# Fused attention and mixture of experts: the weight preparation of six experts moves from the attention into the first token pass, whose second layer becomes plain

## The chip, the cores and the metric

The program runs on one core of one Trainium2 chip. The metric is device time in microseconds (us) of the whole program; lower is better. Three runs of the kernel before gave 1906.63, 1915.39 and 1919.79 us (median 1915.39). One further run was executed under the hardware profiler: 1914.67 us, with a span of 1912.9 us from its first to its last instruction.

## The reference

Causal attention with a decaying bias for 4 batches, 8 heads, 576 positions, head size 64; its output, as 2304 tokens of 512 numbers, goes through eight experts, all of which see every token:

```python
scores = scale * q @ k.T                      # (4, 8, 576, 576), causal
attn   = softmax(scores + min(-(cum_i - cum_j), 0))
x      = (attn @ v) laid out as (2304, 512)
P      = exp(x @ w_gate - max)                # (2304, 8)
for _ in range(8):                            # Sinkhorn: rows, then columns
    P /= P.sum(1) + 1e-9;  P /= P.sum(0) + 1e-9;  P *= N / E
for e in range(8):
    h    = max(x @ w1[e], 0)                  # (2304,512) @ (512,1024)
    out += P[:, e:e+1] * (h @ w2[e])          # (2304,1024) @ (1024,512)
```

## The kernel before

**Numbers.** Every factor is kept as a high part (a cast) and a low part (original minus cast), and a product is three matmuls: high by high, high by low, low by high. A "split" is therefore a cast on ACT and a subtraction on POOL or DVE (helper `sub`, L234; additions L237).

**Attention** (L671 to L712) runs over 80 slots (batch, head pair, row tile), software-pipelined. Between the slots, `fill` drips in matmuls of expert 0, computed plainly (`g1_half` L130, first layer; `g2_chunk` L159, second layer), and `prep` drips in jobs.

**The jobs** prepare the first-layer weights of experts 1 to 7. A unit is a quarter of an expert (256 of 1024 hidden columns), so there are 28. For each, `w1_prep` (L239) loads the raw weights, forms four sums `t13`, `t24` (tile `sb`) and splits three raw blocks and four sums into a tile `w7`, which one DMA stores to the DRAM tensor `w1d`. `w7` and the raw tile `sa` have one buffer each.

**Seven products for eight.** Experts 1 to 7 run in three passes of 768 tokens. Both layers multiply 2x2 blocks with seven products in place of eight, as Strassen and Winograd do. The first layer needs the prepared weights and four sums of token blocks S1 to S4, which `x_sums` (L289) makes from the token blocks in DRAM (`xd`) and stores there. `step1` (L851) is one product of a unit: six matmuls of 384 columns, weights loaded from `w1d` five steps ahead (`load_w1`). Its seventh step also forms sums of the hidden activations: four `clip_op` on DVE and four splits (`plain_split`). `step2` (L951) is one product of the second layer for 128 tokens: twelve matmuls of 256 columns; an expert has 21 of them in a pass, and 28 `step1`. The sums of the second-layer weights are made by `w2_prep` (L269) in the first pass and stored to `w2d`; all second-layer operands are split again for each pass (`split_w2` L931).

**What stands between attention and pass 0.** After the slots, the jobs left over and `x_sums` for pass 0 run (L717 to L720); the attention's pools close; SP, the queue that issues nearly all DMAs in order, is given the seven token loads (`load_x`, L985) and five weight loads, and then the loads of the remaining raw weights of expert 0 (`w_load_early`, L620, tile `wraw`, split at L102/L103). Expert 0's last visits 12 to 15 (batch 3) run beside the Sinkhorn steps (L993).

**Order.** The framework schedules instructions with a timeline simulation of its own; program order is a priority. Each engine then executes its list in order, and a wait holds up all behind it.

Of the kernel before, what the change touches and what calls it, by code (L numbers as in the profile page):

```python
# [14 lines left out]
P = 128  # L15
# [19 lines left out]
TP = 384  # L35
# [3 lines left out]
WOPS = ["11", "21", "22", "T1", "T3", "T2", "T4"]  # L39
XRAW = ["11", "12", "21", "22"]  # L40
# [4 lines left out]
def fused_kernel(ctx: ExitStack, tc: tile.TileContext, qT, kT, v, s, w_gate, wu, out):  # L45
# [193 lines left out]
    def w1_prep(pool, u):  # L239
# [4 lines left out]
        t13 = pool.tile([P, 2, 2, P], F32, name="sb", tag="sb", bufs=2)  # L244
        t24 = pool.tile([P, 2, 2, P], F32, name="sb", tag="sb", bufs=2)
# [19 lines left out]
        parts(5, 2, t24)  # L265
        nc.sync.dma_start(out=w1d[u], in_=w7.bitcast(F32))
        yield

    def w2_prep(pool, u):  # L269

        e, n = divmod(u, UPE)
        r = pool.tile([P, 2, DM], F32, name="sa", tag="sa")
        nc.sync.dma_start(out=r.rearrange("p f d -> p (f d)"), in_=wu[u, :, 1024:2048])
        yield
        t13 = pool.tile([P, 2, DH], F32, name="sb", tag="sb", bufs=2)
        t24 = pool.tile([P, 2, DH], F32, name="sb", tag="sb", bufs=2)
        sub(t13, r[:, :, DH:], r[:, 0, :].rearrange("p (j d) -> p j d", d=DH))
        yield
        sub(t24[:, 0], t13[:, 0], r[:, 1, DH:])
        add(t24[:, 1], t24[:, 0], r[:, 1, :DH])  # L280
        for o, t in ((0, t13), (2, t24)):
            nc.sync.dma_start(
                out=w2d[e][o : o + 2, :, n, :].rearrange("t p d -> p t d"), in_=t
            )
        yield

    XS = 192

    def x_sums(pool, p, k, th, eng):  # L289

        ts = slice(th * XS, (th + 1) * XS)
        x = pool.tile([P, 4, 2, XS], F32, name="sa", tag="sa")
# [3 lines left out]
        ta = pool.tile([P, XS], F32, name="sc", tag="sc", bufs=2)  # L296
        tb = pool.tile([P, XS], F32, name="sc", tag="sc", bufs=2)

        def parts(o, src):
            t = pool.tile([P, 2, XS], F32R, name="sb", tag="sb", bufs=2)  # L300
            nc.scalar.copy(t[:, 0], src)
            sub(t[:, 1], src, t[:, 0].bitcast(F32), eng)
            nc.sync.dma_start(out=xd[p, o][:, :, k, ts], in_=t.bitcast(F32))
# [14 lines left out]
        ta = pool.tile([P, XS], F32, name="sc", tag="sc", bufs=2)  # L318
        add(ta, x[:, 1, 0], tb, eng)
        add(ta, ta, x[:, 1, 1], eng)  # L320
        parts("S4", ta)
        yield
# [325 lines left out]
    def fill(ti):  # L648
# [7 lines left out]
    PREP0, PREP1 = 10, NS - 2  # L656
    jobs = chain(
        [w1_prep(stage, u) for u in range(UPE, NU)]
    )
    njobs = 5 * (NU - UPE)  # L660
    done = [0]

    def prep(ti):
        due = njobs * (ti - PREP0 + 1) // (PREP1 - PREP0)
        while done[0] < min(due, njobs):
            next(jobs, None)
            done[0] += 1

    xs0 = chain([x_sums(stage, 0, k, th, nc.vector) for k in range(2) for th in range(2)])
# [47 lines left out]
    for _ in jobs:  # L717
        pass
    for _ in xs0:
        pass  # L720
    actx.close()

    late = ctx.enter_context(tc.tile_pool(name="late", bufs=1, reuse_waits="tile"))
    ps1 = ctx.enter_context(
# [100 lines left out]
    hops = {}
    hp = []
# [3 lines left out]

    def relu_split(n, o, z):
        t = hp[0].tile([P, 2, TP], F32R, name="h", tag="h", bufs=32)
# [18 lines left out]
    def step1(si):  # L851
        load_w1(si + LEAD1)
        n, o = steps1[si]
        w = w1s.pop(si)
        idx, ui = divmod(n, UPE)
        p = items[idx][0]
# [56 lines left out]

    PROD = ["11", "T1", "T2", "21", "T3", "22", "T4"]
    HOF = {"11": "11", "T1": "S1", "T2": "S2", "21": "12", "T3": "S3", "22": "S4", "T4": "22"}
    steps2 = [(idx, o) for idx in range(NI) for o in PROD]
    r2, w2s = {}, {}
# [67 lines left out]
    for o in XOPS:  # L985
        load_x(0, o)
# [92 lines left out]
```

## Time and profile before

| | |
|---|---|
| profiled execution | 1914.67 us, span 1912.9 us |
| busy: PE, DVE, ACT, POOL | 1702.7, 1307.1, 906.1, 1131.2 us |
| stretch 50 to 425 us (attention) | PE 328.28 of 375 us busy, clock 0.93 |
| stretch 452 to 542 us | PE 2.36 of 90 us busy |
| stretch 650 to 1100 us (pass 0) | PE 415.19 of 450 us busy |
| stretch 1100 to 1900 us (passes 1, 2) | PE 794.67 of 800 us busy |

Busy shares are means over stages with different limits, so the table goes by stage. PE is TensorE; the granted clock is a share of 2.4 GHz, averaged over the stretch.

### The profile page before, as it was taken

How to read it: one execution, taken by the hardware profiler on the slowest of the kernel's cores; microseconds unless marked ns; L12 is line 12 of the kernel's file. 1: busy time of each engine (PE TensorE's matmuls, PEld its weight loads, DVE VectorE, ACT ScalarE, POOL GpSimd, SP SyncE). 2: the span in 40 equal slices, each digit the busy share in tenths (PEclk: the TensorE clock that was granted, in tenths of full speed). 3: DMA queues.
4: the chain of work that ended last, by engine and by line, in shares of the span. 5: the costliest groups of instructions: out<-in, count | busy, mean ns of one | idle time of the engine just before them, and what ended most of it. 6: DMA issues, size and time to landing. Idle time of an engine off the chain costs nothing.

```text
span 1912.9 us, 33715 instructions
## 1 busy us (share of the span) xinstructions
PE 1702.7 (89%) x11865; PEld 1623.9 (85%) x11865; DVE 1307.1 (68%) x2424; ACT 906.1 (47%) x1946; POOL 1131.2 (59%) x993
## 2 busy tenths in 40 slices
PE   5799887994068989989889999999999999999998
PEld 4578776884068989989889999999999999999998
DVE  6668556654326857657767787777787677877775
ACT  5777637653124434434444544444444544444442
POOL 4888677666044666668976454445545444545454
PEclk9799997997579999999999999999999999999999
DMA  6888858875678788877768765665668756656552
GB/s 158 249 261 287 263 208 293 268 263 198 208 284 292 230 263 247 254 249 251 252 219 316 252 186 180 184 186 177 188 187 294 253 175 187 186 179 190 179 181 101
DMA packets 232888, 429.35 MB, mean 224 GB/s; under 512 B 21584, under 2 KB 110160, under 8 KB 229104
## 3 DMA queue, kind: packets, MB, share of 16 engines
q1 hardware_dynamic: 232400, 426.60, 69.5%
q8 instruction: 95, 1.56, 0.3%
q10 hardware_dynamic: 320, 0.59, 0.1%
q14 instruction: 73, 0.60, 0.1%
HBM read 327.01 MB, written 94.81 MB: 221 GB/s over the span
## 4 chain that ended last, share of the span: by engine, by line
PE 49%; DMA 16%; DVE 12%; POOL 12%; issue 6%; SPq 2%; ACT 2%; POOLq 0%; DVEq 0%; ACTq 0%
PE c L869 19%; PE zz L963 12%; PE y L963 8%; DVE s L847 3%; POOL w2o L234 3%; DMA rawq<-qT 3%; DMA sa<-wu 3%; DVE h L234 2%; PE g L167 2%; POOL sb L234 2%; DMA w1d<-w 2%; PE g L138 2%; POOL w L234 2%; POOL h L234 2%; DMA sa<-xd 2%
## 5 line engine op out<-in xcount | busy, mean ns | idle before, releaser
L234 POOL TENSOR_TENSOR w2o<-r,w2o 128x512 fp32r<-128x512 f32 x294 | 419.5, 1447 | 416.1 <-ACT w2o L935 416.1
L869 PE MATMUL c<-xS,w1o 128*128 128x384 f32 x2016 | 423.2, 343 | 21.6 <-DVE z L237 10.8
L963 PE MATMUL zz<-w2o,h 128*128 128x256 f32 x3024 | 424.9, 283 | 9.8 <-POOL w2o L234 6.3
L963 PEld LDWEIGHTS zz<-w2o,h 128*128 128x128 f32 x3024 | 406.6, 189 | 12.4 <-POOL w2o L234 7.8
L869 PEld LDWEIGHTS c<-xS,w1o 128*128 128x128 f32 x2016 | 344.8, 191 | 29.2 <-DVE z L237 14.2
L963 PE MATMUL y<-w2o,h 128*128 128x256 f32 x2268 | 313.8, 284 | 14.6 <-POOL w2o L234 6.8
L963 PEld LDWEIGHTS y<-w2o,h 128*128 128x128 f32 x2268 | 297.8, 189 | 22.8 <-DVE a L978 10.1
L869 PE MATMUL c<-x,w1o 128*128 128x384 f32 x1512 | 306.1, 337 | 4.0 <-ACT c L900 2.7
L833 ACT ACTIVATE h<-z 128x384 fp32r<-128x384 f32 x252 | 131.0, 525 | 296.4 <-DVE z L237 292.1
L869 PEld LDWEIGHTS c<-x,w1o 128*128 128x128 f32 x1512 | 256.5, 188 | 5.4 <-ACT c L900 3.5
L234 POOL TENSOR_TENSOR h<-s,h 128x384 fp32r<-128x384 f32 x168 | 203.3, 1217 | 70.5 <-ACT h L842 69.6
L842 ACT CAST h<-s 128x384 fp32r<-128x384 f32 x336 | 168.0, 513 | 124.7 <-DVE s L847 123.1
L834 DVE SCALAR_TENSOR_TENSOR h<-z,h 128x384 fp32r<-128x384 f32 x252 | 184.4, 740 | 57.9 <-ACT h L833 55.6
L847 DVE SCALAR_TENSOR_TENSOR s<-z,c 128x384 f32<-128x384 f32 x168 | 150.5, 896 | 87.7 <-ACT c L900 87.7
L935 ACT CAST w2o<-r 128x1024 fp32r<-128x1024 f32 x147 | 153.7, 1046 | 86.6 <-PE y L963 56.6
L234 DVE TENSOR_TENSOR h<-s,h 128x384 fp32r<-128x384 f32 x168 | 177.1, 1070 | 3.7 <-ACT h L842 3.1
L978 DVE SCALAR_TENSOR_TENSOR a<-zz,prob,a 128x256 f32<-128x256 f32 x252 | 119.9, 477 | 86.0 <-PE zz L963 85.2
L978 DVE SCALAR_TENSOR_TENSOR a<-y,prob,a 128x256 f32<-128x256 f32 x252 | 113.2, 477 | 85.2 <-PE y L963 84.9
L847 DVE SCALAR_TENSOR_TENSOR s<-z,s 128x384 f32<-128x384 f32 x168 | 165.0, 982 | 2.4
L234 POOL TENSOR_TENSOR sb<-sa 128x512 f32<-128x512 f32 x56 | 74.7, 1334 | 148.0 <-DMA sa<-wu 142.7
L237 DVE TENSOR_TENSOR z<-c,t 128x384 f32<-128x384 f32 x252 | 136.6, 548 | 32.4 <-PE c L869 28.8
L505 ACT ACTIVATE T<-T,mn 128x128 f32<-128x128 f32 (+2 forms) x144 | 83.6, 581 | 50.0 <-DVE mn L473 39.2
(133 smaller groups left out, 2337.9 us busy)
## 6 DMA issues: line engine op xcount, KB each, us to landing
w1o<-w1d SPq DMA_DIRECT2D x588, 256.0 KB
w1d<-w SPq DMA_DIRECT2D x28, 1792.0 KB
r<-w2d SPq DMA_DIRECT2D x84, 512.0 KB
r<-wu SPq DMA_DIRECT2D x63, 512.0 KB
sa<-wu SPq DMA_DIRECT2D x56, 512.0 KB
w2d<-sb SPq DMA_DIRECT2D x56, 256.0 KB
wraw<-wu SPq DMA_DIRECT2D x44, 256.0 KB
rawq<-qT SPq DMA_DIRECT2D x64, 144.0 KB
```

Of the source, the lines that this page charges most:

```text
L138: nc.tensor.matmul(ps[:, :n], lhsT=w1[:, w, o : o + P], rhs=xcols(b, x, k, n0, n), start=(k == 0 and t == 0), stop=(k == KD - 1 and t == 2),)
L234: (eng or nc.gpsimd).tensor_tensor(out=out, in0=a, in1=b, op=ALU.subtract)
L237: (eng or nc.gpsimd).tensor_tensor(out=out, in0=a, in1=b, op=ALU.add)
L505: nc.scalar.activation(T[:, :n], T[:, :n], AF.Exp, bias=mn[:, 1:2], scale=-1.0, accum_out=sums[t][:, j : j + 1],)
L833: nc.scalar.activation(t[:, 0], z, AF.Relu)
L834: nc.vector.scalar_tensor_tensor(out=t[:, 1], in0=z, scalar=0.0, in1=t[:, 0].bitcast(F32), op0=ALU.max, op1=ALU.subtract,)
L842: nc.scalar.copy(t[:, 0], z)
L847: nc.vector.scalar_tensor_tensor(out=out, in0=z, scalar=0.0, in1=other, op0=ALU.max, op1=op)
L869: nc.tensor.matmul(ps, lhsT=w[:, wl, k], rhs=x[:, xl, k], start=(fresh and k == 0 and t == 0), stop=(k == 1 and t == 2), skip_group_check= ...
L935: nc.scalar.copy(w[:, :, 0], r)
L963: nc.tensor.matmul(ps, lhsT=h[:, a, ci * P : (ci + 1) * P], rhs=w[:, ui, b_], start=(fresh and ui == 0 and t == 0), stop=(ui == UPE - 1 an ...
L978: nc.vector.scalar_tensor_tensor(out=a, in0=ps, scalar=prob[:, c, e : e + 1], in1=a, op0=ALU.mult, op1=ALU.add)
```

## The change

Only expert 1's four units are still prepared in the attention (`NPRE = UPE`). The token sums of passes 0 and 1 become attention jobs on POOL (from slots 44 and 64), those of pass 2 run in pass 0 on DVE. The first-layer weights of experts 2 to 7 are made one unit ahead of their use in pass 0 (`w1_ahead`), in four groups held in a ring of seven tiles `wp`, consumed directly and also stored to `w1d` for passes 1 and 2. The second layer of pass 0 is plain (`step2p`): per expert 24 steps of six matmuls of 512 columns, weights split by `prep_w2`, which also stores the sums for later passes. Pass 0's seventh `step1` is a plain `relu_split`. Passes 1 and 2 keep their steps. `x_sums` and `w1_prep` issue a store one job step later than before. The seven token loads and the first weight loads are issued one per step of expert 0's last visits.

```diff
+WGRP = [(0, 2), (2, 1), (3, 2), (5, 2)]
+NPRE = UPE
-    def w2_prep(pool, u):
...
-    PREP0, PREP1 = 10, NS - 2
-    jobs = chain([w1_prep(stage, u) for u in range(UPE, NU)])
-    njobs = 5 * (NU - UPE)
+    PREP0, PREP1 = 16, NS - 2
+    xs = lambda p: [x_sums(stage, p, k, th, 192, nc.gpsimd) for k in range(2) for th in range(2)]
+    plan = [(0, 6, w1_prep(stage, u)) for u in range(UPE, UPE + NPRE)]
+    plan += [(44, 6, g) for g in xs(0)] + [(64, 6, g) for g in xs(1)]
+    jobs = [(t, g) for t, n, g in plan for _ in range(n)]
...
-    xs0 = chain([x_sums(stage, 0, k, th, nc.vector) for k in range(2) for th in range(2)])
...
+    def w1_group(n, g):
+        o, k = WGRP[g]
+        t = p0.tile([P, 2, 2, 2, P], F32R, name="wp", tag="wp", bufs=7)
...
+    def w1_make(n, g, src):
+        t = w1_group(n, g)
+        hi, lo = t[:, :k, 0], t[:, :k, 1]
+        nc.scalar.copy(hi, src)
+        sub(lo, src, hi.bitcast(F32))
+    def w1_ahead(n, q):
+        if NPRE <= n + 2 < NUP and q == 0:
+            w1_raw(n + 2)
+        n += 1
+        if n < NPRE:
+            g = {0: 0, 2: 2, 4: 1, 5: 3}.get(q)
+            if g is not None:
+                w1_fetch(n, g)
+            return
+        r = raw1.get(n)
+        if q == 0:
+            w1_make(n, 0, r[:, :, 0, :].rearrange("p (o k) c -> p o k c", k=2))
+            t13 = p0.tile([P, 2, 2, P], F32, name="sb", tag="sb", bufs=4)
+            sub(t13, ..., nc.vector)
+        elif q == 1:
+            sub(t24[:, 0], sums1[n][:, 0], r[:, 2:4, 1, :], nc.vector)
+            add(t24[:, 1], t24[:, 0], r[:, 2:4, 0, :], nc.vector)
+        elif q == 2:
+            w1_store(n, 0)
+            w1_make(n, 2, sums1.pop(n))
...
+        elif n < NUP:
+            relu_split(n, "21", ps)
...
+    def prep_w2(m):
+        r = r2.pop(m)
+        for f in range(NFC):
+            w = hp[2].tile([P, 2, DM], F32R, name="w2p", tag="w2p", bufs=9)
+            split(w[:, 0], w[:, 1], r[:, f])
+        sub(t13, r[:, :, DH:], r[:, 0, :].rearrange("p (j d) -> p j d", d=DH), nc.vector)
+        sub(t24[:, 0], t13[:, 0], r[:, 1, DH:], nc.vector)
+        add(t24[:, 1], t24[:, 0], r[:, 1, :DH], nc.vector)
+        for o, t in ((0, t13), (2, t24)):
+            nc.sync.dma_start(out=w2d[e][...], in_=t)
+        load_r2(m + 2)
...
+    def step2p(idx, i, ui, ci):
+        if ui == 0:
+            zb[ci] = ps2.tile([P, 512], F32, name="zz", tag="zz", bufs=3)
+        for f in range(NFC):
+            h, w = hops[m, f"{i + 1}{f + 1}"], w2p[m, f]
+            for t, (a, b_) in enumerate(((0, 0), (0, 1), (1, 0))):
+                nc.tensor.matmul(zb[ci], lhsT=h[:, a, ci * P : (ci + 1) * P], rhs=w[:, b_], ...)
+        if ui == UPE - 1:
+            gated(c, e, accs[c], zb[ci])
...
-    for o in XOPS:
-        load_x(0, o)
-    for si in range(LEAD1):
-        load_w1(si)
...
     while stream.queue:
         stream.step()
+        if k < 7:
+            load_x(0, XOPS[k])
+        if 7 <= k < 11:
+            w1_fetch(0, (0, 2, 1, 3)[k - 7])
+        k += 1
```

**SP between attention and pass 0.** `sa<-xd` and `xd_S<-sb` are `x_sums`' loads and stores, `w1d<-w` a unit's store, L797 (before) and L788 (after) are `load_x`. Before, from the last two units of `w1_prep`:

```order
L242 DMA sa<-wu 128x1024
L266 DMA w1d_124<-w_5362 128x3584
L294 DMA sa<-xd_11_74 128x2x192
L294 DMA sa<-xd_12_75 128x2x192
L294 DMA sa<-xd_21_76 128x2x192
L294 DMA sa<-xd_22_77 128x2x192
L266 DMA w1d_125<-w_5491 128x3584
L303 DMA xd_S_78<-sb 256x1x192
L303 DMA xd_S_80<-sb 256x1x192
```

Behind these stand three more rounds of `sa<-xd` and `xd_S<-sb`, then the seven L797 loads, five of `w1o<-w1d`, and only then the first `wraw<-wu`. With the change:

```order
L93 DMA xd_22_93<-xl 128x2x384
L788 DMA x_5775<-xd_11_74 128x1536
L788 DMA xS_5795<-xd_S_78 128x1536
L788 DMA x_5808<-xd_12_75 128x1536
L788 DMA xS_5822<-xd_S_81 128x1536
L788 DMA xS_5834<-xd_S_79 128x1536
L182 DMA accd_144<-acc 128x512
L788 DMA xS_5848<-xd_S_80 128x1536
L788 DMA x_5861<-xd_22_77 128x1536
L836 DMA wp<-w1d_98 128x1024 x2
L836 DMA wp<-w1d_98 128x512
L617 DMA wraw<-wu 128x512 x2
```

The stores of the last token rows (L93) are followed at once by the token loads, and one unit's weights stand between these and `wraw`; no unit of `w1_prep` and no `x_sums` is left there.

**PE in pass 0.** First-layer steps (`c<-`) and second-layer steps (`y`, `zz`), before:

```order
L963 MATMUL zz<-w2o,h 128x256 x14
L869 MATMUL c<-x_6042,w1o 128x384 x6
L963 MATMUL zz<-w2o,h 128x256 x3
L869 MATMUL c<-xS_6046,w1o 128x384 x6
L963 MATMUL zz<-w2o,h 128x256 x12
L869 MATMUL c<-x_6038,w1o 128x384 x6
```

and with the change, at the pass's end (`x_10287` is a token block of pass 1):

```order
L1053 MATMUL zz<-w2p,h 128x512 x7
L946 MATMUL c<-x_5808,wp 128x384 x6
L946 MATMUL c<-xS_5848,wp 128x384 x6
L1053 MATMUL zz<-w2p,h 128x512 x18
L946 MATMUL c<-x_5861,wp 128x384 x6
L1053 MATMUL zz<-w2p,h 128x512 x72
L946 MATMUL c<-x_10287,w1o 128x384 x6
```

The weights come from `wp`, the second layer has rows of 512 columns, and the last 72 of these stand alone before pass 1's first step.

## Rows read from the trace of the kernel before

**Rows 1.** Stages: stretch, us; busy PE, PEld, DVE, ACT, POOL; clock, DMA share, GB/s.
```profile
50.00:425.00 375.00, 328.28 (x2528) 281.17 (x2528) 239.89 (x673) 249.50 (x679) 288.07 (x261) 0.93 0.80 261
425.00:452.00 27.00, 25.71 (x151) 23.39 (x150) 16.71 (x41) 10.27 (x22) 14.62 (x14) 1.00 0.58 229
452.00:542.00 90.00, 2.36 (x9) 1.98 (x10) 26.20 (x73) 12.47 (x30) 20.36 (x20) 0.51 0.65 235
576.00:650.00 74.00, 64.52 (x394) 62.79 (x393) 56.31 (x78) 32.23 (x65) 41.88 (x35) 0.98 0.84 270
650.00:1100.00 450.00, 415.19 (x2799) 405.45 (x2798) 305.51 (x476) 193.95 (x377) 318.27 (x306) 0.98 0.79 255
1100.00:1900.00 800.00, 794.67 (x5563) 786.45 (x5561) 613.27 (x955) 366.08 (x673) 397.78 (x294) 1.00 0.61 190
```
**Rows 2.** PE's waits from 460 us: total us, times, longest.
```profile
PE c L138 <- ACT w L102: 79.0, 1, 79.0
```
**Rows 3.** Chain of waits, pieces between attention and pass 0: start, us, what.
```profile
464.31 4.40 POOL w L234 x4
...
475.35 1.95 POOL w L234 x2
479.26 2.90 DMA sa<-xd
...
522.63 11.09 DMA xS<-xd_S
533.73 7.22 DMA wraw<-wu
```
**Rows 4.** Timeline of PE, first matmul of pass 0.
```profile
575.97 1.21 PE L869 MATMUL c<-x,w1o 128*128 128x384 f32 x6
```
**Rows 5.** Chain of waits, runs of matmuls back to back, count behind x.
```profile
553.16 2.76 PE c L167 x12
...
1131.48 2.11 PE c L869 x12
...
1138.70 1.43 PE y L963 x12
...
1191.88 2.11 PE c L869 x12
```
**Rows 6.** SP's and DVE's waits, 50 to 430 us: total us, times, longest.
```profile
SPq L242 <- POOL w L234: 41.0, 13, 10.1
DVE qa L426 <- DMA rawq<-qT: 20.5, 15, 3.2
```
**Rows 7.** Groups on POOL: count, busy us, mean ns of one, idle before.
```profile
L234 POOL TENSOR_TENSOR sb<-sa 128x512 f32<-128x512 f32 x56 | 74.7, 1334 | 148.0 <-DMA sa<-wu 142.7 <-DMA w1o<-w1d 5.0
L234 POOL TENSOR_TENSOR w<-sb,w 128x512 fp32r<-128x512 f32 x56 | 72.3, 1305 | 0.9 <-ACT w L252 0.4
L234 POOL TENSOR_TENSOR sb<-sb,sa 128x256 f32<-128x256 f32 x56 | 45.3, 809 | 3.0
L234 POOL TENSOR_TENSOR w<-sa,w 128x256 fp32r<-128x256 f32 x28 | 21.7, 773 | 0.1
L237 POOL TENSOR_TENSOR sc<-sc,sa 128x192 f32<-128x192 f32 x24 | 16.6, 693 | 0.6
```
**Rows 8.** Groups on DVE and one on ACT, the same columns.
```profile
L834 DVE SCALAR_TENSOR_TENSOR h<-z,h 128x384 fp32r<-128x384 f32 x252 | 184.4, 740 | 57.9 <-ACT h L833 55.6
L234 DVE TENSOR_TENSOR h<-s,h 128x384 fp32r<-128x384 f32 x168 | 177.1, 1070 | 3.7 <-ACT h L842 3.1
L847 DVE SCALAR_TENSOR_TENSOR s<-z,s 128x384 f32<-128x384 f32 x168 | 165.0, 982 | 2.4
L237 DVE TENSOR_TENSOR z<-c,t 128x384 f32<-128x384 f32 x252 | 136.6, 548 | 32.4 <-PE c L869 28.8 <-ACT t L879 3.2 <-ACT t L885 0.3
L237 DVE TENSOR_TENSOR sc<-sa 128x192 f32<-128x192 f32 x8 | 2.9, 358 | 30.3 <-DMA sa<-xd 30.3
L252 ACT CAST w<-sb 128x512 fp32r<-128x512 f32 x56 | 32.5, 615 | 0.0
```

More of the change, by code (lines that the diff above doesn't have):

```diff
@@ L265, in w1_prep, with x_sums @@
         parts(5, 2, t24)
+        yield
         nc.sync.dma_start(out=w1d[u], in_=w7.bitcast(F32))
         yield
[L269 to L292 removed]
+    def x_sums(pool, p, k, th, n, eng):
+        ts = slice(th * n, (th + 1) * n)
+        x = pool.tile([P, 4, 2, n], F32, name="sa", tag="sa", bufs=1 if n == 192 else 2)
         for i, o in enumerate(XRAW):
@@ L716, in fused_kernel @@
         stream.step()
[L717 to L720, printed above, removed]
+    for _, g in jobs:
+        next(g, None)
     actx.close()
     late = ctx.enter_context(tc.tile_pool(name="late", bufs=1, reuse_waits="tile"))
+    p0ctx = ctx.enter_context(ExitStack())
+    p0 = p0ctx.enter_context(tc.tile_pool(name="p0", bufs=1, reuse_waits="tile"))
     ps1 = ctx.enter_context(
@@ new lines, in fused_kernel, with load_acc, store_out, gated @@
+    accs = {}
+    def load_acc(p):
+        for j in range(6):
+            c = 6 * p + j
+            accs[c] = late.tile([P, DM], F32, name="a", tag="a", bufs=6)
+            nc.sync.dma_start(out=accs[c], in_=accd[c])
+            nc.scalar.activation(accs[c], accs[c], AF.Copy, scale=prob[:, c, 0:1])
+    def store_out(c):
+        nc.sync.dma_start(out=out[c * P : (c + 1) * P, :], in_=accs.pop(c))
+    def gated(c, e, a, ps):
+        nc.vector.scalar_tensor_tensor(
+            out=a, in0=ps, scalar=prob[:, c, e : e + 1], in1=a, op0=ALU.mult, op1=ALU.add
+        )
@@ L1001, in fused_kernel, with run1 @@
         pass
+    bctx.close()
+    p0ctx2 = ctx.enter_context(ExitStack())
+    hp[:] = [
+        p0ctx2.enter_context(tc.tile_pool(name=n, bufs=1, side="right", reuse_waits="tile"))
+        for n in ("h0", "w2x")
+    ]
+    hp.insert(1, None)
+    load_r2(0)
+    load_r2(1)
+    NS1 = 7 * UPE
+    si = 0
+    def run1(upto):
+        nonlocal si
+        while si < min(upto, len(steps1)):
+            step1(si)
+            si += 1
+    run1(NS1 - 8)
+    load_acc(0)
+    run1(NS1 - 4)
+    for m in range(3):
+        prep_w2(m)
@@ new lines, in fused_kernel, with plain_item @@
+    run1(NS1 - 2)
+    side = chain(
+        [x_sums(p0, 2, k, th, 128, nc.vector) for k in range(2) for th in range(3)]
+    )
+    last = E - 2
+    pace = float(si)
+    def plain_item(idx):
+        nonlocal pace
+        for i in range(2):
+            for ui in range(UPE):
+                ahead = (
+                    UPE * idx + 3 if (i, ui) == (0, 0)
+                    else UPE * (idx + 1) + ui - 1 if i == 1 and ui
+                    else None
+                )
+                if ahead is not None and ahead != NUP - 1:
+                    prep_w2(ahead)
+                for ci in range(3):
+                    if idx < last:
+                        pace += 28 / 24
+                        run1(min(int(pace), NS1P))
+                        if idx >= 2:
+                            next(side, None)
+                    step2p(idx, i, ui, ci)
```

217 lines of the change are left out of this document (144 added, 73 removed).

## The prediction

> **What bounds the kernel now.** I read the busy shares by stage first, because the means over the whole span hide three regimes [rows 1]. In the attention (50 to 425 us) PE is busy 328 of 375 us, with POOL at 288: a mixture of waits. From 452 to 542 us PE does next to nothing, 2.36 us in 90. Pass 0 runs with PE at 415 of 450, and passes 1 and 2 with PE at 795 of 800. So only what lies before 1100 us can be shortened by moving work; after that only fewer or shorter matmuls help.
>
> PE's waits name the hole: one wait of 79.0 us for the cast of a raw weight of expert 0 [rows 2]. The chain of waits shows why so small a load is late [rows 3]: at 475 us POOL still ends the last unit of weight preparation, from 479 us the token sums of pass 0 are loaded, computed and stored in turn, at 522 us the stored sums are loaded back (11.09 us), and the raw weight stands behind them on the same queue (7.22 us). It has landed at 541 us, where PE goes on; pass 0 begins at 575.97 us [rows 4].
>
> **The sum.** I rebuild the span: the start of pass 0, then steps times their prices, then what is lost between them. Prices are runs of matmuls that follow each other without a gap [rows 5]: twelve of 384 columns 2.11 us, so a first-layer step of six is 1.05; twelve of 256 columns 1.43 to 1.44, a second-layer step before; twelve of 512 columns 2.76, so a plain step of six is 1.38. The same point of two successive experts in pass 1 lies at 1131.48 and 1191.88 us: 60.4 us, against 28 x 1.05 + 21 x 1.44 = 59.6, so 0.8 us an expert are lost even there.
>
> *Check on before.* 588 first-layer steps x 1.05 = 617, 441 second-layer steps x 1.44 = 635, 21 x 0.8 = 17: 1269 us. From 576 us to the end at 1912.9 it took 1337. The other 68 us are starts, tail and stalls; about 10 of them I put to the second half, where PE idles 5 us of 800 [rows 1] and then runs down its tail. That leaves 58 for pass 0, of which PE's idle time shows 9.5 (576 to 650) and 34.8 (650 to 1100); the rest I read as the clock of 0.98 and short breaks inside busy stretches.
>
> *Start of pass 0.* (a) The hole. The work that fills it (the last three units, four blocks of sums) leaves the place, as SP's order shows. What still stands ahead of the raw weight is seven token blocks of 768 KB and 1.75 MB of weights, 7 MB. Before, the same seven blocks and 1.25 MB of weights were under way from 522 us and the raw weight behind them had landed at 541 [rows 3]: some 20 us. They can start when the attention's last tiles are done, and PE then has the two visits of expert 0 that it did from 425 to 452 us, 27 us. So I keep 4 us of the 90 and gain 86. Without that cover up to 20 us would come back; below zero is excluded, since the matmuls behind it need the load. (b) The attention. POOL loses 21 units there (the last ones end at 469 and about 480 us, 11 us apart [rows 3], so 25 of 28 were done by 452; 4 stay) of 7.6 us each (1.33 + 2 x 0.81 + 3 x 1.30 + 0.77 [rows 7]), 160 us, and gains 8 blocks of sums, 13 operations of about 0.7 us each [rows 7], 73 us. ACT loses three casts a unit at 0.6 us [rows 8] and a shorter one. SP loses 41.0 us of standing still until POOL frees the single raw tile, with the query loads queued behind, for which DVE waited 20.5 us [rows 6]. It gains 64 small loads and stores. PE idles 47 us in this stretch, at a clock of 0.93 [rows 1]. How much of that is due to the jobs no row says: nothing at least, or even 10 us to the bad if the 64 DMAs delay the heads' loads in their turn; all 47 at most. I take 20, near the waits of SP and DVE just named. Pass 0 then starts at 576 - 86 - 20 = 470.
>
> *Steps.* First layer 617 as before. Second layer: 294 steps of passes 1 and 2 x 1.44 = 423, and 7 experts x 24 plain steps x 1.38 = 232, which took 147 x 1.44 = 212 before. So the plain layer **costs** PE 20 us. Small breaks 17 as before. Together 1289.
>
> *Losses kept.* (c) The start of pass 0 draws four units of prepared weights (7 MB) and 2.5 MB of second-layer weights within 28 steps, 29 us, where the same stage moved 270 GB/s [rows 1]: 35 us, so 6 lost, I take 8. (d) The first 28 steps of pass 1 now stand alone, as those of pass 0 did, and there DVE sets the pace: a unit there is 3 x 0.55 + 3 x 0.74 + 4 clips at up to 0.98 + 2 x 1.07 = 9.9 us [rows 8] against 7.4 of PE; 4 units, 10 us lost. Under the 72 plain matmuls that end pass 0 (17 us) the new token blocks load, so I add nothing for them. (e) Inside pass 0 a unit now takes PE 7 x 1.05 + 6 x 1.38 = 15.6 us. POOL does 3 subtractions of 512 columns, one of 256 and two of `prep_w2`, 7.5 us [rows 7]; ACT 7 evictions and 6 casts of 0.6 at most, 8 us; DVE 3 x 0.55 + 4 x 0.74 for the unit, two sums of 512 and four of 256, at the rates of 358 ns for 192 columns or 1070 for 384 [rows 8] 3.8 to 5.7 us, and 1.4 of gated additions, together 10 to 12 with 1 to 2 more for the sums of pass 2. Every engine has a quarter free, which was not so for POOL before (318 of 450 us busy, plus waits). I keep 10 us of the 58. (f) Tail and turn to pass 2: 10, unchanged.
>
> Sum: 470 + 1289 + 8 + 10 + 10 + 10 = 1797, and 1.8 us between span and time: **1800**. Against the profiled 1914.67 that is 115 us or 6%; that execution lies at the median of the three runs, 1915.39. With (a) at 0 to 20, (b) at -10 to 47 and (e) at 0 to 30 this case reaches from 1768 to 1836.
>
> **A rule against the change.** The weight sums move from POOL to DVE while POOL subtracts. Rows show what such neighbours cost: a DVE subtraction of 384 columns takes 1070 ns in the passes, 2.8 ns a column, while one of 192 took 358, 1.9 a column, in the hole, where POOL was all but idle [rows 8]. I have priced the sums at both.
> The Trainium skill (SBUF — State Buffer, "Who interferes with whom") says that a DVE instruction with two inputs in SBUF and a GpSimd instruction that reads SBUF exclude each other for a whole instruction; by that the loss would be larger than a slower column rate, and it is the second rival below. The slowdown of the 1070 ns row agrees with such an exclusion in part of the cases.
>
> **Rivals.** *Only the hole closes.* The attention is bound by its own chain from scores to softmax to transposes, and keeps its 20 us; pass 0 keeps 45 of its 58 us, now from w1 groups that arrive late. 1800 + 20 + 35 = 1855. For it: PE's waits in the attention cost little each; against it: the 41 us of SP.
>
> *DVE is blocked in pass 0.* If each of a unit's six sums first sits out a POOL subtraction of 1.3 us, DVE needs 11 + 6 x 1.3 = 18.8 us against PE's 15.6: 3 us for each of 24 units, 1872. Against it: POOL is busy only half of the time, so hardly every sum can meet one.
>
> *Slower: the ring of seven.* A group is made a unit ahead and held 8 to 13 steps; four groups hold 46 steps of the 49 that seven tiles offer in a unit. So each ACT cast waits for PE's last read of an older group, and the evictions that PE needs stand behind it on ACT. If every group then shows PE its cast and subtraction (0.6 + 1.3 = 1.9 us), 4 x 1.9 = 7.7 us a unit over 24 units are 184: 1984. It is slower than before from 4.8 us a unit. Against it: a freed tile is wanted only some six steps later, 13 us.
>
> *The hole stays in part,* since token blocks and weights still stand ahead of the raw weight and land late: 20 to 30 us, 1825.
>
> **How the numbers follow.** Chances: forecast 0.64, only the hole 0.17, DVE blocked 0.09, hole in part 0.05, slower by the ring 0.04, and 0.01 for the rest. The range runs from 1768 to 1858: all but a little of the forecast's own range, the part hole, and most of the first rival; outside lie DVE blocked, the ring and the tails, about 0.2. The bound between no change and a change is 1%, 19 us, about what runs that spread over 13 us can tell. Only the ring reaches beyond it upward (0.04); no change takes the 0.01 and the far ends of the rivals that stall pass 0 (0.03 in all); what is left, 0.93, is faster.
>
> **What would show it.** PE's longest wait after 400 us is under 20 us, and pass 0 begins near 470 us. Successive experts of pass 0 lie 63 us apart, with PE over 95% busy, and those of passes 1 and 2 60.4 as now. At the start of pass 1 PE idles some 10 us on DVE. I am wrong if pass 0 shows PE waiting on POOL or ACT for `wp`, if an expert takes over 70 us there, or if a wait for `wraw` of tens of us remains.

## Result and the profile after

The changed kernel takes **1813.42 us** (median of four runs, 1808.13 to 1815.89), the kernel before 1913.09 in the same session (1906.63 to 1919.79). The ratio is 0.9475, with a 95% interval of 0.9434 to 0.9516: faster by 100 us, 13 us short of the forecast. The profiled execution took 1815.05 us, span 1813.3, at a mean clock of 0.979.

The stages of the changed kernel, with the columns of [rows 1] (stretch, its length; busy PE, PEld, DVE, ACT, POOL; clock, DMA share, GB/s):

```profile
50.00:425.00 375.00, 334.34 (x2562) 283.72 (x2563) 223.85 (x679) 227.24 (x636) 206.91 (x228) 0.94 0.61 186
425.00:452.00 27.00, 27.00 (x157) 24.58 (x156) 16.56 (x46) 6.99 (x15) 2.54 (x2) 1.00 0.88 342
452.00:485.00 33.00, 28.93 (x136) 24.80 (x135) 17.89 (x36) 9.75 (x19) 7.75 (x6) 0.90 0.33 112
485.00:690.00 205.00, 200.64 (x1002) 182.01 (x1001) 114.81 (x181) 82.89 (x170) 91.72 (x72) 0.98 0.61 209
690.00:930.00 240.00, 220.14 (x1066) 195.10 (x1065) 149.97 (x269) 91.67 (x196) 101.94 (x80) 0.98 0.68 227
930.00:956.00 26.00, 24.89 (x115) 20.90 (x115) 7.06 (x12) 5.47 (x9) 5.03 (x4) 1.00 0.89 307
956.00:1040.00 84.00, 81.84 (x526) 80.09 (x525) 62.84 (x101) 42.93 (x84) 28.78 (x22) 1.00 0.65 197
1040.00:1800.00 760.00, 755.58 (x5292) 748.10 (x5291) 580.55 (x903) 348.00 (x638) 377.47 (x279) 1.00 0.61 191
```

The 90 us with 2.36 us of PE are gone: from 425 to 485 us PE now idles 4 of 60. In the attention POOL fell from 288 to 207 us and the DMA share from 0.80 to 0.61, and yet PE gained only 6 us there. The new row to look at is 690 to 930 us, where PE idles 20 of 240 and the clock shows no more than 0.98. The two rows from 956 us on idle 6.6 us of 844 together.

Where each stage begins is read from one line's matmuls: operation, count, ns min/median/max, first and last start, form. `wp` is pass 0, `w1o` passes 1 and 2:

```profile
L946 PE MATMUL c<-x,w1o x1008: 331/334/346, 957.3 to 1781.9; 128*128 128x384 f32 x168
L946 PE MATMUL c<-x,wp x504: 332/334/686, 485.0 to 940.8; 128*128 128x384 f32 x168
```

So pass 0 runs from 485.0 (before 575.97 [rows 4]) to 957.3 us, 472.3 us, and passes 1 and 2 take the 856.0 us to the span's end. All runs below are split in the same three numbers.

PE's waits from 400 to 1100 us (who waits, for whom: total us, times, longest) against the 79.0 us of [rows 2]:

```profile
PE c L946 <- DVE h L911: 11.7, 4, 4.4
PE c L946 <- DVE z L239: 5.4, 5, 2.4
PE zz L1053 <- ACT w2p L104: 4.4, 1, 4.4
PE zz L1053 <- DVE a L1039: 3.3, 2, 2.7
...
PE c L946 <- ACT wp L852: 0.7, 1, 0.7
```

DVE is the engine that is late, with evictions (`h`, `z`) that are short work in themselves. Its own waits from 690 to 820 us say why:

```profile
DVE sc L239 <- DMA sa<-xd: 12.2, 6, 3.1
DVE h L911 <- ACT h L910: 6.8, 4, 4.0
DVE sb L236 <- DMA w2d<-sb: 6.8, 3, 4.0
```

`sc` is the first addition of a block of pass 2's token sums: DVE stands still six times until the block (`sa`) has landed, and the evictions that PE needs stand behind it in DVE's order. The chain of waits in this stretch (start, us, what) alternates between the same names:

```profile
706.79 2.63 DMA sa<-xd
...
717.60 6.72 DMA w2d<-sb
724.42 1.21 DVE sb L236
725.63 1.56 DVE h L911
...
729.42 2.89 DMA sa<-xd
```

### The profile page after: what moved, and what is told of

Its sections match the earlier page's. It is cut to its first block, busy times and chain, and to the rows that moved or that the text cites. A ratio compares the mean times of both kernels' runs of the same rounds, so it can differ in the third digit from the quotient of the medians.

```text
span 1813.3 us, 31303 instructions
## 1 busy us (share of the span) xinstructions
PE 1713.0 (94%) x11109; PEld 1592.5 (88%) x11109; DVE 1211.8 (67%) x2340; ACT 845.2 (47%) x1849; POOL 852.0 (47%) x739
## 4 chain that ended last, share of the span: by engine, by line
PE 61%; DVE 14%; DMA 13%; issue 4%; POOL 4%; ACT 2%; SPq 2%; DVEq 0%; POOLq 0%; ACTq 0%
PE c L946 25%; PE zz L1104 11%; PE zz L1053 9%; PE y L1104 7%; DVE s L922 3%; DMA w2d<-sb 3%; DMA rawq<-qT 2%; PE g L169 2%; PE g L140 2%; DVE h L236 2%; DVE sb L236 2%; DMA sa<-xd 1%; PE sc L458 1%; DVE h L911 1%; PE pv L560 1%
## 5 line engine op out<-in xcount | busy, mean ns | idle before, releaser
L236 POOL TENSOR_TENSOR w2o<-r,w2o 128x512 fp32r<-128x512 f32 x196 | 280.1, 1452 | 386.9 <-ACT w2o L1087 386.9
L946 PE MATMUL c<-xS,w1o 128*128 128x384 f32 x1344 | 277.8, 339 | 3.4 <-DVE z L239 1.6
L1104 PE MATMUL zz<-w2o,h 128*128 128x256 f32 x2016 | 280.1, 282 | 0.0
L1104 PEld LDWEIGHTS zz<-w2o,h 128*128 128x128 f32 x2016 | 269.4, 188 | 0.4 <-ACT h L910 0.2
L1053 PE MATMUL zz<-w2p,h 128*128 128x512 f32 x1008 | 249.6, 395 | 7.7 <-ACT w2p L104 4.4
L946 PEld LDWEIGHTS c<-xS,w1o 128*128 128x128 f32 x1344 | 226.5, 188 | 7.5 <-DVE z L239 2.8
L1053 PEld LDWEIGHTS zz<-w2p,h 128*128 128x128 f32 x1008 | 189.3, 189 | 44.1 <-ACT w2p L104 5.0
L1039 DVE SCALAR_TENSOR_TENSOR a<-zz,prob,a 128x256 f32<-128x256 f32 (+1 forms) x210 | 110.2, 530 | 82.8 <-PE zz L1104 53.0
L946 PE MATMUL c<-xS,wp 128*128 128x384 f32 x672 | 133.8, 341 | 4.3 <-DVE z L239 3.5
L946 PEld LDWEIGHTS c<-xS,wp 128*128 128x128 f32 x672 | 121.4, 192 | 9.5 <-DVE z L239 4.4
```

Source lines behind the costliest of these rows:

```text
L236: (eng or nc.gpsimd).tensor_tensor(out=out, in0=a, in1=b, op=ALU.subtract)
L946: nc.tensor.matmul(ps, lhsT=w[:, wl, k], rhs=x[:, xl, k], start=(fresh and k == 0 and t == 0), stop=(k == 1 and t == 2), skip_group_check= ...
L1039: nc.vector.scalar_tensor_tensor(out=a, in0=ps, scalar=prob[:, c, e : e + 1], in1=a, op0=ALU.mult, op1=ALU.add)
L1053: nc.tensor.matmul(zb[ci], lhsT=h[:, a, ci * P : (ci + 1) * P], rhs=w[:, b_], start=(ui == 0 and f == 0 and t == 0), stop=(ui == UPE - 1 a ...
L1104: nc.tensor.matmul(ps, lhsT=h[:, a, ci * P : (ci + 1) * P], rhs=w[:, ui, b_], start=(fresh and ui == 0 and t == 0), stop=(ui == UPE - 1 an ...
```

## Experiments

Each kernel is split as above, from its profiled execution (us):

| kernel | pass 0 begins | pass 0 lasts | passes 1 and 2 | median of runs |
|---|---|---|---|---|
| changed | 485.0 | 472.3 | 856.0 | 1813.42 |
| e2, hardly any jobs in the attention | 452.8 | 471.3 | 856.0 | 1781.34 |
| e6, units kept, sums of passes 0 and 1 out | 460.7 | 469.2 | 856.4 | 1789.54 |
| e3, sums of pass 2 out | 482.9 | 447.7 | 857.5 | 1790.13 |
| e11, their arithmetic out | 480.5 | 464.0 | 856.7 | 1803.20 |
| e4, two rings of sums | 481.6 | 475.8 | 854.9 | 1816.08 |
| e5, sums of pass 2 on POOL | 483.6 | 467.1 | 855.9 | 1808.46 |
| e10, spread over pass 0 | 484.0 | 479.4 | 856.6 | 1822.07 |
| e7, on POOL in pass 1 | 484.9 | 446.4 | 869.8 | 1802.49 |
| e8, e7 with pass 1's sums in pass 0 | 462.8 | 472.6 | 868.5 | 1809.81 |
| e9, e7 spread over pass 1 | 482.9 | 445.8 | 863.9 | 1795.65 |
| e12, ring of six `wp` tiles | 478.1 | 486.3 | 856.2 | 1825.99 |

In nine of these kernels (the changed one, e3, e4, e5, e7, e9 to e12) the attention is the same program, and pass 0 begins between 478.1 and 485.0 us. So a difference of up to 7 us in the first column says nothing by itself; the third column, where nothing behind pass 0 was changed, agrees to 3 us.

### Was the hole the work that filled it? (e1)

The kernel before, without the work that ends in the hole:

```diff
-        [w1_prep(stage, u) for u in range(UPE, NU)]
+        [w1_prep(stage, u) for u in range(UPE, NU - 3)]
...
-    xs0 = chain([x_sums(stage, 0, k, th, nc.vector) for k in range(2) for th in range(2)])
+    xs0 = chain([])
...
```

> The kernel before, with the work that fills the stretch between attention and pass 0 left out: the last three units' first-layer weights (another unit's are read instead) and the token sums of pass 0 (raw token blocks are read). Everything else as before, also the order token loads, weight loads, raw weight on SP. Theory (the work itself was the hole, the loads behind it are covered by two visits): the wait of 79 us shrinks to 0 to 10 us and the time falls by 75 to 90 us, to about 1830. Rival (the loads ahead of the raw weight make a hole of their own): 20 to 35 us of the wait stay, time about 1855.

Measured: 1841.51 us (1837.96 to 1848.11), ratio 0.9626 (0.9602 to 0.9651), 70 us less, between the theory's 1830 and the rival's 1855. Its stage where the hole was, and two pieces of its chain of waits:

```profile
452.00:480.00 28.00, 8.91 (x35) 7.47 (x36) 7.91 (x24) 6.12 (x10) 5.18 (x5) 0.63 1.01 393
```
```profile
451.70 13.03 DMA xS<-xd
464.74 7.24 DMA wraw<-wu
```

Pass 0 begins at 508.5 us. So the fill was some 68 of the 90 us, and 19 us of idle time stay (28 minus 8.91) while the DMA engines are full at 393 GB/s: the raw weight still stands behind the token blocks. In the changed kernel 342 GB/s are moved from 425 to 452 us beside expert 0's last visits, and PE is busy all the time. That the fill was the larger part is shown by e1; that the cover is worth the rest is read by comparing the two kernels, which differ in more than this order.

### What holds the attention? (e2, e6)

e2, the changed kernel with one unit prepared and no sums for passes 0 and 1:

```diff
-    plan = [(0, 6, w1_prep(stage, u)) for u in range(UPE, UPE + NPRE)]
-    plan += [(44, 6, g) for g in xs(0)] + [(64, 6, g) for g in xs(1)]
+    plan = [(0, 6, w1_prep(stage, u)) for u in range(UPE, UPE + 1)]
...
```

> The changed kernel, with the attention's jobs left out but for one unit: three of expert 1's four units are not prepared (the one is read for all four), and the token sums of passes 0 and 1 are not made (raw blocks are read). Theory (the attention is bound by its own chain of scores, softmax and transposes, so jobs cost it little): the first matmul of pass 0 comes at most 8 us before the 485 us of the changed kernel, time 1805 to 1813. Rival (POOL and DMA jobs still held it up, as the forecast of 20 us supposed): 15 to 30 us earlier, time 1785 to 1798.

e6 takes out the line of sums alone and keeps the four units:

```diff
-    plan += [(44, 6, g) for g in xs(0)] + [(64, 6, g) for g in xs(1)]
...
```

> The changed kernel with expert 1's four units prepared in the attention, and the token sums of passes 0 and 1 left out (raw blocks are read). Leaving out three units and all sums gave 1781 us, with expert 0's last visits starting 31 us earlier. In that run 14 us of these were already there at the eighth of sixteen row-tile groups, before the sums begin. Theory (both count, about by their work on POOL, 23 us of units against 73 of sums): visits start 15 to 20 us earlier than the 419 us of the changed kernel, time 1793 to 1800. Rival (the units' 1.75 MB stores and raw loads in front of the query loads are what hurts): visits start under 8 us earlier, time over 1804.

Measured: e2 1781.34 us (1780.34 to 1782.60), ratio 0.9318 (0.9303 to 0.9334); e6 1789.54 (1787.40 to 1791.65), ratio 0.9352 (0.9326 to 0.9379). From 50 to 400 us, columns as above, the changed kernel:

```profile
50.00:400.00 350.00, 310.35 (x2375) 263.00 (x2376) 213.00 (x655) 222.31 (x624) 206.91 (x228) 0.93 0.61 184
```

e6, without the sums:

```profile
50.00:400.00 350.00, 323.42 (x2562) 277.58 (x2562) 222.97 (x680) 217.18 (x606) 147.55 (x125) 0.96 0.53 163
```

and e2, with hardly any job:

```profile
50.00:400.00 350.00, 326.03 (x2605) 280.30 (x2606) 222.82 (x689) 214.72 (x598) 125.29 (x103) 0.98 0.50 151
```

Pass 0 begins 24 us earlier without the sums and 8 us earlier still without the other three units; the rest of the program keeps its length to some 3 us. Both times lie a little below the ranges that had these jobs cost something (1785 to 1798 and 1793 to 1800). The theory that the attention is bound by its own chain is refuted: what remains of the jobs costs 32 us. The sums are 59 us of POOL (206.91 minus 147.55), which is nowhere near full; nothing here tells their POOL work from their 64 small DMAs.

The cost is not all waiting. From 50 to 425 us the changed kernel does 2562 matmuls (first table), as many as e6 does from 50 to 400. They keep PE busy for 334.34 and for 323.42 us: of the 25 us between the two, 11 are matmuls that took longer, at a granted clock of 0.94 against 0.96, and 14 are idle time. DVE's wait for the query block, which I had named before, does not follow the gain: 21.9 us from 50 to 400 us in the changed kernel, 17.3 in e6, 10.5 in e2.

### What stalls pass 0? (e3, e4, e5, e10, e11)

e3 leaves pass 2's sums out:

```diff
-        [x_sums(p0, 2, k, th, 128, nc.vector) for k in range(2) for th in range(3)]
+        []
...
```

> The changed kernel without the token sums of pass 2 (raw blocks are read), so without their loads, DVE sums, ACT casts and stores in pass 0. Theory (DVE stands still in order for the loads of those sums and for free sum tiles, and PE then waits for DVE): PE's idle time from 690 to 930 us falls from 21 to under 8 us, time 1796 to 1803. Rival (the stores of the second-layer weight sums hold DVE, and they stay): idle time falls by less than 6 us, time 1808 to 1813.

Measured: 1790.13 us (1788.47 to 1792.25), ratio 0.9364 (0.9348 to 0.9381). The theory called it, and the gain is 6 us more than its range. Pass 0 shrinks by 24.6 us, to 447.7, and from 690 to 914 us PE idles only 3.6. Six blocks of sums, 78 operations of about 0.3 us on DVE, 23 us in all, cost PE as much again. All of pass 0, in the changed kernel and in e3:

```profile
485.00:957.00 472.00, 446.67 (x2184) 398.85 (x2183) 272.60 (x463) 180.51 (x376) 198.69 (x156) 0.98 0.66 223
```
```profile
483.00:930.60 447.60, 438.85 (x2185) 395.14 (x2184) 256.87 (x385) 175.76 (x353) 199.21 (x156) 0.99 0.65 222
```

Here too a third of the price is no wait: idle time falls from 25.3 to 8.8 us, and the same matmuls take 7.8 us less, at a granted clock of 0.99 against 0.98.

e4 gives the second-layer sums a ring of their own, since in the chain a `w2d` store holds a `sb` tile that a sum waits for (three and two tiles in place of four shared ones):

```diff
-        t13 = p0.tile([P, 2, DH], F32, name="sb", tag="sb", bufs=4)
-        t24 = p0.tile([P, 2, DH], F32, name="sb", tag="sb", bufs=4)
+        t13 = p0.tile([P, 2, DH], F32, name="sw", tag="sw", bufs=2)
+        t24 = p0.tile([P, 2, DH], F32, name="sw", tag="sw", bufs=2)
...
```

> The changed kernel with the ring of four sum tiles of pass 0 split in two: three for first-layer weight sums and token sums, two for the second-layer weight sums, whose stores free their tiles late. Theory (the shared ring makes one kind of sum wait for the stores of the other): PE's idle time in pass 0, 25 us, falls by 5 to 12 us, time 1801 to 1808. Rival (DVE runs in order, so it stands still in front of a second-layer sum all the same, now with two tiles in place of four): no gain or up to 10 us slower, 1813 to 1823.

Measured: 1816.08 us (1809.71 to 1826.61), ratio 0.9505 (0.9468 to 0.9542): no gain, as the rival said. DVE's waits from 560 to 900 us, first in the changed kernel:

```profile
DVE sb L236 <- DMA w2d<-sb: 21.6, 16, 4.0
DVE sc L239 <- DMA sa<-xd: 15.8, 8, 3.1
...
DVE sb L236 <- DMA sa<-wu: 8.0, 4, 3.5
```

and in e4, where the wait for the store only moved, to the next transfer:

```profile
DVE sw L236 <- DMA r<-wu: 36.1, 12, 4.9
```

e5 makes the same sums on POOL:

```diff
-        [x_sums(p0, 2, k, th, 128, nc.vector) for k in range(2) for th in range(3)]
+        [x_sums(p0, 2, k, th, 128, nc.gpsimd) for k in range(2) for th in range(3)]
```

> The changed kernel with one engine changed: the token sums of pass 2, still made in pass 0, run on POOL and not on DVE. Leaving them out gave 1790 us. Theory (PE waits because DVE, in order, stands still for the loads and stores of these sums; POOL has half of pass 0 free and PE needs it less directly): most of the 23 us come back, time 1792 to 1800. Rival (the sums cost by their DMAs and sum tiles, whichever engine makes them; POOL then stands still and the weight groups come late): time 1806 to 1820.

Measured: 1808.46 us (1806.72 to 1809.43), ratio 0.9450 (0.9425 to 0.9476): the rival's range; 5 us of pass 0's 25 come back. DVE no longer waits for the token blocks. ACT, which casts the sums, waited 15.2 us for DVE's from 690 to 930 us in the changed kernel, and waits longer for POOL's:

```profile
ACT sb L285 <- POOL sc L239: 29.8, 16, 5.0
```

ACT makes evictions too, so whichever engine takes the sums, one that PE depends on stands still.

e11 keeps the loads and stores and leaves the arithmetic out:

```diff
+        x = pool.tile([P, 4, 2, n], F32, name="sa", tag="sa", bufs=2)
+        for i, o in enumerate(XRAW):
+            nc.sync.dma_start(out=x[:, i], in_=xd[p, o][:, :, k, ts])
...
+            nc.sync.dma_start(out=xd[p, o][:, :, k, ts], in_=x[:, i])
```

> The changed kernel with pass 2's token sums left out, while their 24 loads and 24 stores stay (the loaded blocks are stored as they are, so pass 2 computes with raw blocks in place of sums). If the arithmetic on DVE, and its standing still for the loads, is what costs 23 us, the time comes near that of e3, 1788 to 1794; if it is SP's queue and the transfers, near the changed kernel's, 1806 to 1814.

Measured: 1803.20 us (1802.69 to 1805.17), ratio 0.9423 (0.9404 to 0.9443), and pass 0 464.0 us. Between both theories: of pass 0's 24.6 us, 16.3 stay with the transfers alone and 8.3 go with the arithmetic; by the medians of the runs it is 13 and 10. So transfers without any arithmetic cost more than half. From 560 to 900 us DVE waits in e11 for two older customers of SP's queue:

```profile
DVE sb L236 <- DMA w2d<-sb: 24.7, 20, 4.1
DVE sb L236 <- DMA sa<-wu: 20.8, 9, 4.2
```

In e3 these two were 17.3 and 12.3 us: the raw weights share the ring of two `sa` tiles with the token blocks, and their loads are issued behind SP's waits. But e11 is harder on that ring than the changed kernel: its stores read `sa` itself and hold it until they have read it, where `x_sums` stores from `sb`. In the changed kernel the wait for the raw weights is 8.0 us, less than in e3, and what is new there is the wait of 15.8 us for the blocks. So 16 us is at most what SP's queue and the transfers cost; how it divides is not shown.

e10 spreads the sums over pass 0. Written order is only a priority for the scheduler, so a copy of one column of a prepared weight into the tile ties each block to a place:

```diff
+        if gate:
+            nc.gpsimd.tensor_copy(out=x[:, 0, 0, 0:1], in_=gate())
...
+    gate = lambda: list(grp.values())[-1][:, 0, 1, 0:1].bitcast(F32)
-                        if idx >= 2:
+                        if ci == 0:
```

> The changed kernel with the token sums of pass 2 still on DVE in pass 0, but each block tied to a prepared first-layer weight, so that the six blocks spread over 36 of pass 0's second-layer steps from its first expert on (some 370 us), instead of lying in 90 us around 700 to 790 us. Theory (bunching): DVE no longer stands still for blocks that follow one another, most of the 23 us of e3 comes back, 1793 to 1800. Rival (the amount of work, or one wait per block wherever it lies): 1808 to 1816.

Measured: 1822.07 us (1819.77 to 1826.31), ratio 0.9522 (0.9501 to 0.9543): worse, pass 0 at 479.4, and above the range of either. Spreading brought no gain, and DVE's wait for the blocks stayed, 14.9 us against 15.8 from 560 to 900 us:

```profile
DVE sc L239 <- DMA sa<-xd: 14.9, 8, 4.0
```

But e10 does not settle bunching, since the tie has a price of its own. From 485 to 930 us SP's queue, with all loads behind it, stands still six times for the copy on POOL that lets a block load:

```profile
SPq L279 <- POOL sa L277: 30.0, 6, 6.8
```

### Where do the sums cost least? (e7, e8, e9)

e7 makes them on POOL beside pass 1, with one `sa` tile:

```diff
...
+    side2 = chain(
+        [x_sums(hp[1], 2, k, th, 128, nc.gpsimd, 1) for k in range(2) for th in range(3)]
+    )
...
+            if i < 49 and (3 * i + ci) % 3 == 0:
+                next(side2, None)
```

> The changed kernel with the token sums of pass 2 moved from pass 0 on DVE to pass 1 on POOL, one job step per second-layer product. Theory (DVE in pass 0 was the cause, and POOL in passes 1 and 2 is half free with PE at 99%): the gain of leaving them out, 23 us, is kept but for 0 to 5 us: 1790 to 1796. Rival (POOL stands still for their loads in front of the second-layer splits that PE waits for): pass 1 loses 10 us or more, time over 1800.

e8 moves, besides, pass 1's sums from the attention into pass 0, on POOL:

```diff
-    plan += [(44, 6, g) for g in xs(0)] + [(64, 6, g) for g in xs(1)]
+    plan += [(44, 6, g) for g in xs(0)]
...
-        [x_sums(p0, 2, k, th, 128, nc.vector) for k in range(2) for th in range(3)]
+        [x_sums(p0, 1, k, th, 128, nc.gpsimd) for k in range(2) for th in range(3)]
...
```

> As the run before (pass 2's sums in pass 1 on POOL), and also the token sums of pass 1 moved from the attention into pass 0, on POOL, two job steps in three. The attention keeps four units and the sums of pass 0. Theory (each block of sums costs the attention about 2 us; POOL has room in pass 0): visits start 6 to 10 us earlier, pass 0 loses under 3 us, time 1782 to 1790. Rival (the sums hold POOL in pass 0 and the weight groups come late, as in the run on POOL if that is slow): no gain over the run before, 1792 to 1805.

e9 is e7 with each block tied to a second-layer weight of pass 1, as in e10 (here against e7):

```diff
+    gate = lambda: w2s[i][:, 0, 1, 0:1].bitcast(F32)
...
-            if i < 49 and (3 * i + ci) % 3 == 0:
+            if 2 <= i < 49 and ci == 1:
```

> The changed kernel with the token sums of pass 2 made on POOL in pass 1, as in e7_sums2_pass1, but each of the six blocks may load only once POOL has written the second-layer weight of a given step (a copy of one column into the tile ties them), so that the blocks spread over 38 steps of pass 1, some 330 us, and do not all stand in its first 100 us. Theory (the same work costs nothing when it is thin, and costs PE what it does when it stands bunched where DMAs and POOL are needed at once): pass 0 stays as short as in e7 (446 us) and passes 1 and 2 return from 870 to 857-860 us, 1787 to 1793 in all. Rival (the price is that of the work and its 48 DMAs wherever they stand): 1800 as e7.

Measured: e7 1802.49 us (1800.07 to 1802.87), ratio 0.9417 (0.9392 to 0.9443); e8 1809.81 (1805.65 to 1810.56), ratio 0.9460 (0.9430 to 0.9490); e9 **1795.65** (1794.38 to 1799.46), ratio 0.9385 (0.9365 to 0.9404). e7 comes out by its rival (over 1800): it takes 26 us from pass 0 and gives 14 back in pass 1. Its start of pass 1:

```profile
930.00:1030.00 100.00, 90.25 (x564) 85.46 (x563) 66.71 (x103) 49.30 (x112) 71.71 (x100) 1.00 0.77 238
```

The scheduler had drawn all of e7's sums into the first 100 us of pass 1 (POOL 71.71 us there, 44.60 in e9). From 932 to 1232 us e7, e9 and e3, which has no such sums, compare so:

```profile
932.00:1232.00 300.00, 288.00 (x1934) 281.38 (x1934) 221.15 (x340) 140.76 (x280) 170.92 (x171) 0.99 0.65 200
```
```profile
932.00:1232.00 300.00, 289.85 (x1979) 285.69 (x1978) 224.82 (x352) 142.19 (x280) 166.47 (x168) 1.00 0.66 202
```
```profile
932.00:1232.00 300.00, 297.70 (x2038) 294.44 (x2037) 231.35 (x359) 142.18 (x268) 137.40 (x103) 1.00 0.62 189
```

Spread, the sums cost less: 863.9 us against 869.8, where none at all is 857.5. That is part of what the theory asked for, and e9 missed its range by 3 us. It beats both kernels, the changed one by some 17 us (0.9385 against 0.9475).

e8 gains 22 us in the attention and loses 26 in pass 0 against e7, above the ranges of its theory and its rival. Beside e6 it says more. With pass 0's sums alone in the attention pass 0 begins at 462.8 us (e8), with no sums at 460.7 (e6), with both at 485.0: so the first four blocks, made from some 190 to 265 us, cost next to nothing (2 us), and the next four, the same operations from some 320 to 395 us, cost some 20. A price per block would have had both wrong.

### The ring of seven (e12)

```diff
-        t = p0.tile([P, 2, 2, 2, P], F32R, name="wp", tag="wp", bufs=7)
+        t = p0.tile([P, 2, 2, 2, P], F32R, name="wp", tag="wp", bufs=6)
```

> The changed kernel with six instead of seven tiles in the ring of prepared first-layer weights of pass 0. The rival of the prediction (ACT's cast waits for PE's last read of an older group, and evictions stand behind it) counts 46 steps held of 49 offered; six tiles offer 42, so by it every group would be late and show PE 1.9 us and more: 4 x 1.9 x 24 = 184 us, near 2000. Theory (a freed tile is wanted so much later that the cast still comes in time): under 20 us, 1813 to 1833.

Measured: 1825.99 us (1822.38 to 1829.31), ratio 0.9539 (0.9517 to 0.9562): 13 us more, in the theory's range. From 485 to 940 us ACT stands longer for PE's last read in e12:

```profile
ACT wp L852 <- PE c L946: 146.5, 50, 5.7
```

than in the changed kernel:

```profile
ACT wp L852 <- PE c L946: 109.2, 56, 5.7
```

Yet PE waits for no `wp`. Its waits in pass 0 are for evictions, 30 us in e12 against 17 (5.2 and 11.7) in the changed kernel:

```profile
PE c L946 <- DVE z L239: 15.3, 13, 2.3
PE c L946 <- DVE h L911: 14.8, 7, 5.0
```

So the first half of the rival's mechanism is seen, and one tile short of seven costs 13 us, not 184. That the evictions are late because they stand behind the cast fits these waits, but is not shown step by step.

## Why the prediction was right, and where it was not

The time lay 13 us above the forecast, well inside the range, and no rival's time was reached. That it came so near is partly luck, since errors of 13 us and more cancel in part. Step by step, against the profile's span:

- **(a) The hole**: 86 of 90 us predicted, 4 kept. Visits 12 of expert 0 begin at 418.8 us and pass 0 at 485.0: 66.2 us for work that took 26.3 and 34.3 us on either side of the hole before, so 6 kept. Right, and the cover was needed: in e1 some 20 us stay.
- **(b) The attention**: 20 us predicted, 7 measured (visits 12 at 418.8, before at 425.7; between 415 and 422 us in the nine kernels with this attention). This is the term that failed most, by 13 us. I took the waits of SP and DVE as the sign of relief and gave the incoming sums 10 us at the worst and none in the sum. With the sums out visits 12 begin at 395.3 us (e6): what left the attention was worth 30 us, and what came in took 24 of them back. The three other units are another 8 (e2).
- **The steps' prices** held. In the chain of waits, runs of second-layer matmuls of 512 columns, an expert apart:

```profile
543.11 3.67 PE zz L1053 x16
...
605.47 3.67 PE zz L1053 x16
```

  Sixteen in 3.67 us are 1.38 for six, as predicted, and the same run comes back after 62.4 us (63 predicted), with 168 first-layer and 144 second-layer matmuls between, those of one expert. At this price the plain layer does cost PE its 20 us.
- **(c) and (e), pass 0**: 462 us predicted (206 + 232 + 5.6 + 8 + 10), 472.3 measured. Two errors hide in the difference. Without pass 2's sums pass 0 takes 447.7 (e3), 14 less than I allowed: three engines with a quarter free do hold the pace. With the sums it takes 24.6 more, where I had covered them by that free quarter. PE was to be over 95% busy and was 94.6 (446.67 of 472). A busy share of 0.6 on DVE covers work, but not standing still in order for a transfer.
- **(d) The start of pass 1**: 10 us predicted; over its first 30 us PE idles 1.8, and DVE, which was to set the pace, is busy little more than half:

```profile
957.00:987.00 30.00, 28.22 (x167) 27.19 (x166) 16.28 (x26) 15.82 (x34) 4.80 (x4) 1.00 0.73 227
```

  The 28 steps do not stand alone, as I had it. After the sixth PE does second-layer matmuls of pass 1 between them, the first of them here:

```profile
963.59 1.24 PE L1104 MATMUL zz<-w2o,h 128*128 128x256 f32 x9
```

- **(f) and the passes**: 856.0 us against 866 predicted (392 x 1.05 + 423 + 11 + 10 + 10). Most of the difference is (d).

Sum of the misses: +2, +13, +11, -10, which is +16 on the predicted span of 1797. One sum of mine was off as well: with (a), (b) and (e) all at their ends the forecast's own case reaches from 1759 to 1866, not from 1768 to 1836. The measured time lies inside both. And the row of 192 columns that I set beside a subtraction [rows 8] is an addition.

**The rivals.** *Only the hole closes* (1855): its half on the attention came near, since only 7 of the 20 us were gained, but for another reason than its own chain; its half on pass 0 (groups that arrive late) did not. *The hole in part* (1825): 6 us of it stay, not 20 to 30. *DVE blocked by POOL* (1872): DVE did become the late engine, but by transfers. What the neighbour costs can be read from the first sum of a unit's first-layer weights. By tile, ns min/median/max:

```profile
L236 DVE TENSOR_TENSOR sb<-sa x24: 640/693/1806, 447.3 to 880.5; 128x512 f32<-128x512 f32 x24
```

Sixteen of the 24 take 0.64 to 0.69 us and eight 1.22 to 1.81. Each of the eight began while POOL was inside a subtraction, 0.03 to 0.63 us after its start; none of the sixteen did. One of the eight, and one of the sixteen, which POOL's subtraction follows at once:

```profile
535.51 1.28 POOL L236 TENSOR_TENSOR wp<-sb,wp 128x512 fp32r<-128x512 f32 x1 [1.83 <-ACT wp L852]
535.76 1.58 DVE L236 TENSOR_TENSOR sb<-sa 128x512 f32<-128x512 f32 x1 [1.67 <-DMA sa<-wu]
...
505.00 0.69 DVE L236 TENSOR_TENSOR sb<-sa 128x512 f32<-128x512 f32 x1 [3.46 <-DMA w2d<-sb]
505.01 1.82 POOL L105 TENSOR_TENSOR w2p<-r,w2p 128x512 fp32r<-128x512 f32 x1 [4.56 <-ACT w2p L104]
```

In both pairs the one that starts second takes longer than alone, by about what was left of the first. So the exclusion is seen here both ways, and one such sum in three sits out the rest of a subtraction, not each of the six of a unit. By the rule of the Trainium skill (SBUF — State Buffer, "Who interferes with whom") the later of two such instructions is blocked for the whole of the other. The trace agrees, and how seldom they meet is this kernel's own number. With these meetings a unit's six sums took 4.8 us on average, inside the 3.8 to 5.7 that I had priced. *The ring* (1984): PE waited 0.7 us for `wp` in all, and e12 shows the seventh tile to be worth 13 us.

What stays open: whether POOL work or small DMAs make the sums dear in the attention, and why there only the second four blocks are; how pass 0's 25 us divide between DVE's wait for the blocks, the ring of `sa` and SP's order of issue; and what spreading would do in pass 0 without the waits that e10's tie adds.

## To carry to other kernels

Before small background work is booked as free under an engine's idle share, ask what that engine will stand still for in order, and what PE needs that is queued behind: here 23 us of DVE arithmetic with 48 small transfers cost PE 25 us beside an engine that was 60% busy, a third of it as matmuls that ran longer. Moving such work to another engine of the same stage kept most of its price (20 us on POOL); by place the price of such blocks ran from 2 to 26 us, so a place has to be tried and not booked. It was less in pass 1 (12 us against e3), and there less again where data dependences spread it (6 us), since the scheduler had drawn it together. And when work leaves a stage, price what comes in as carefully as what goes out.

## What the runs showed of the hardware

The token blocks are 128 KB transfers with rows of 512 bytes. From 690 to 820 us they made the changed kernel's DMA line

```profile
DMA packets 21009, 31.16 MB, mean 240 GB/s; under 512 B 1586, under 2 KB 15112, under 8 KB 21000
```

against e3's without them

```profile
DMA packets 11503, 28.04 MB, mean 216 GB/s; under 512 B 1057, under 2 KB 5199, under 8 KB 11495
```

For 11% more bytes there are 83% more packets. The same view gives the hardware queue a share of 72.5% in the changed kernel and of 63.1% in e3. That is 331 and 342 GB/s for a full share, so with the small rows a byte took some 3% more of the DMA engines' time in this stretch. In e1's 28 us of large loads the engines moved 393 GB/s at a share of 1.01.
